# A doubling of lag factors on VectorE with the small power first, and its last step summed by transfers

## The chip, the cores and the metric

The kernel runs on one core of a Trainium2 chip. A core has TensorE (matrix products, with its weight loads shown apart as PEld), VectorE (DVE), ScalarE (ACT), GpSimd (POOL) and SyncE (SP, which issues most transfers). Each engine works through its own queue in order, and waits on semaphores for the others. The metric is the time of one execution on the device in microseconds (us); less is better.

## The reference, cut to what matters

Four layers follow one another on a sequence of 2048 rows of 512 channels: a long convolution, a gated feed-forward, and both once more. The convolution's filter is a sum over 128 states of powers of a complex number:

```
P = exp(logdA[:, :, None] * l)             # [512, 128, 2048], logdA = dt * A
K = einsum("dn,dnl,dn->dl", Cc, P, dB).real
y = irfft(rfft(u, 2L) * rfft(K, 2L))[:L] + u * Dskip
x = x + y
x = x + (silu(n @ w_gate) * (n @ w_up)) @ w_down     # n = layernorm(x)
```

The filter K depends on the weights alone. The kernel computes it once, for both convolutions.

## The kernel before, in words

**The chunk stage.** The filter is built for 8 chunks of 64 channels, with the 128 states on the partitions. A lag l is split as 32 a + s with a below 64 and s below 32. For each chunk the kernel makes two tables: `re` and `im` hold the complex powers in a (64 of them for each channel), `g` holds the 32 small powers in s, multiplied by the weight `w0` = C dt B. `lags` (L449) then multiplies them on TensorE, one small product per channel and part: 32 columns of `g` are the stationary operand, 64 columns of `re` or `im` the moving one, summed over the states. `spread_in`, `spread` and `spectra` (L460 to L518) turn the result into frequency weights: an eviction by ScalarE (L462), a rearranging product that also adds the row `dsk` of Dskip (L474), another eviction to `kt`, the spectral products (L493), their eviction (L502), sums on GpSimd (L504 to L514) and stores by SP (L516).

**The tables.** Sizes are exponentials on ScalarE (`gen_exp`, L384), among them five for the powers 1, 2, 4, 8, 16 of the small factor (`mz`, L389). Angles start on VectorE (`gen_turns`: L349 for 16 large multiples, L352 for the small powers), are rounded by ScalarE (`gen_reduce`: L360, L366), reduced on VectorE (L369, L372), and turned into sine and cosine on ScalarE (`gen_trig`: L379 to L381). `gen_e` (L401) puts `re` and `im` together on VectorE: L407 and L410 for one half, L413 and L416 for the other.

**The doubling.** `gen_g` (L419) multiplies the small factors `xr` and `xi` by their sizes (L424), makes the first factor (L427 to L431), and then doubles the table five times, for n = 1, 2, 4, 8, 16: entries n to 2n - 1 are entries 0 to n - 1 times the n-th power. Each doubling is a product with the real part (L437), one with the imaginary part into a scratch tile `tmp` (L441, at most 8 powers at a time, so twice for n = 16), a subtraction and an addition (L445, L446). `g` is laid out as [part, channel, power]: the 32 powers of a channel are neighbours.

**The order.** The order of the instructions on VectorE, ScalarE and TensorE is written out by hand for this stage: the steps are generators, and the text takes so many steps of each in turn (L850 on; the loop over chunks starts at `for i in range(NCH - 1)`). In turn i of the loop, VectorE makes `g` (`gg`) and the joined tables (`ge`) of chunk i + 1 and the angles (`tn`, `rd`) of chunk i + 2; ScalarE makes sines and exponentials of chunk i + 2 (`tr`, `ex`); TensorE makes the lag products and spectra of chunk i. It also forms norms of the feed-forward weights (`norm_units`, with the squares at L306 and the sums at L310) and the spectra of the second input block (`second`, L276, L279). In the last turn there is no chunk i + 2. The orders of SP's and GpSimd's queues, and of all engines behind this stage, come from a planner that simulates the kernel and issues an instruction when it thinks it is due.

**Buffers.** Tiles share memory by tag: a new tile of a tag waits for the readers of the old one. `bt` is the scratch of `tmp`, and later receives pieces of the feed-forward weights (L572); `t` holds `dsk` until the products of the convolution use it (L683). `W0` to `W3` hold `re` and `im` of even and odd chunks.

**Behind the stage.** The first block's convolution (`ssm`, L640, with `ei` products at L702), then for eight blocks the convolution of the next block on VectorE beside the feed-forward of this one on TensorE (L807 to L823).

Of the kernel before, what the change touches and what calls it, by code (L numbers as in the profile page):

```python
# [22 lines left out]
P = 128  # L23
# [13 lines left out]
NA = 21  # L37
# [7 lines left out]
def dft_constants():  # L45
# [17 lines left out]
    am[:, :5] = 2.0 ** np.arange(5)  # L63
    am[:, 5:] = 32.0 * np.arange(17, 33)
# [8 lines left out]
def kernel(ctx, tc, x, a_re, a_im, b_re, b_im, c_re, c_im, log_dt, d_skip,  # L73
# [25 lines left out]

    ldt = sb.tile([P, 4], F32, name="ldt")  # L100
# [65 lines left out]
    dt = tl([P, D], "dt", "bt")  # L166
# [3 lines left out]
    def gen_w():  # L170

        wt = tl([P, 2, D], "wt", "bt")
# [6 lines left out]
    dsk = tl([1, D], "dsk", "t")  # L179
# [154 lines left out]
    mz2 = tl([P, 2, 5, DC], "mz2", "y1")  # L334

    def gen_tiles(ch):
        re = tl([P, DC, 65], "re", f"W{2 * (ch % 2)}")
        im = tl([P, DC, 65], "im", f"W{2 * (ch % 2) + 1}")
        mu = tl([P, DC, 32], "mu", "n")
        xz = tl([P, 5, DC], "xr", "bb"), tl([P, 5, DC], "xi", "dd")  # L340
        mz = mz2[:, ch % 2]
        t16 = tl([P, DC, 16], "t16", "z")
        return re, im, mu, xz, mz, t16

    def gen_turns(ch, ts):
# [3 lines left out]
        V.tensor_tensor(t16, am[:, 5:].unsqueeze(1).to_broadcast([P, DC, 16]),  # L349
                        t_.unsqueeze(2).to_broadcast([P, DC, 16]), OP.mult)  # L350
        yield
        V.tensor_tensor(xz[1], am[:, :5].unsqueeze(2).to_broadcast([P, 5, DC]), t_.unsqueeze(1).to_broadcast([P, 5, DC]), OP.mult)  # L352
# [31 lines left out]
    def gen_exp(ch, ts):  # L384
# [3 lines left out]
        for lv in range(5):  # L388
            A.activation(mz[:, lv], r_, AF.Exp, scale=float(1 << lv))  # L389
# [29 lines left out]
    def gen_g(ch, ts, g):  # L419
# [6 lines left out]
        tmp = tl([P, 2, DC, 8], "tmp", "bt")  # L426
        V.tensor_tensor(g[:, :, :, 0], w_, re[:, :, 64].unsqueeze(1).to_broadcast([P, 2, DC]), OP.mult)  # L427
        V.tensor_tensor(tmp[:, :, :, 0], w_[:, ::-1], im[:, :, 64].unsqueeze(1).to_broadcast([P, 2, DC]), OP.mult)
        yield
        V.tensor_tensor(g[:, 0, :, 0], g[:, 0, :, 0], tmp[:, 0, :, 0], OP.subtract)  # L430
        V.tensor_tensor(g[:, 1, :, 0], g[:, 1, :, 0], tmp[:, 1, :, 0], OP.add)  # L431
        for n in (1, 2, 4, 8, 16):
            yield
            lv = n.bit_length() - 1
            zr, zi = (t[:, lv].unsqueeze(1).unsqueeze(3) for t in xz)
            new = g[:, :, :, n:2 * n]
            V.tensor_tensor(new, g[:, :, :, 0:n], zr.to_broadcast([P, 2, DC, n]), OP.mult)  # L437
            step = min(n, 8)
            for b0 in range(0, n, step):
                tmp = tl([P, 2, DC, 8], "tmp", "bt")[:, :, :, :step]  # L440
                V.tensor_tensor(tmp, g[:, ::-1, :, b0:b0 + step], zi.to_broadcast([P, 2, DC, step]), OP.mult)  # L441
                if b0 + step == n:
                    yield
                o = new[:, :, :, b0:b0 + step]
                V.tensor_tensor(o[:, 0], o[:, 0], tmp[:, 0], OP.subtract)  # L445
                V.tensor_tensor(o[:, 1], o[:, 1], tmp[:, 1], OP.add)  # L446
        yield

    def lags(ts, g):  # L449
        re, im = ts[:2]  # L450
        pk = pbig([P, 16, 64], "pk")
        for d in range(DC):
# [3 lines left out]
            PE.matmul(o, lhsT=g[:, 0, d], rhs=re[:, d, 0:64], start=True, stop=False, tile_position=(0, 32 * grp))  # L456
            PE.matmul(o, lhsT=g[:, 1, d], rhs=im[:, d, 0:64], start=False, stop=True, tile_position=(0, 32 * grp))
# [388 lines left out]
    with tc.manual_schedule(engines={mybir.EngineType.Activation, mybir.EngineType.DVE, mybir.EngineType.PE}):  # L846
# [18 lines left out]
        gs[0] = tl([P, 2, DC, 32], "g", "ga")  # L865
# [33 lines left out]
        for i in range(NCH - 1):  # L899
# [6 lines left out]
            gs[i + 1] = tl([P, 2, DC, 32], "g", ("gb", "ga")[i % 2])  # L906
# [6 lines left out]
            take(gg, 1)  # L913
            take(tn, 1)
            take(gg, 1)
            take(tn, 1)
# [3 lines left out]
            take(gg, 1)  # L920
            take(ge, 1)
            take(gg, 1)
            take(ge, 1)
            take(gg, 1)
            take(ge, 1)
            take(gg, 1)
            take(ge, 1)
            take(gg, 1)
# [167 lines left out]
```

## Time and profile before

| | before |
|---|---|
| median of 3 runs | 1214.09 us (1213.27 to 1214.4) |
| the profiled execution | span 1210.1 us, from first to last instruction; no other time is given for it |
| TensorE busy | 1104.0 us, 91% |
| VectorE busy | 1048.5 us, 87% |
| ScalarE busy | 646.3 us, 53% |
| GpSimd busy | 187.8 us, 16% |

The runs' time is that of the whole execution; what lies around the span (start and end) is in the first row and not in the second. Shares are averages over the whole span, and the stages have different limits. In rows of a profile, `L441` is a line of the kernel, `tmp<-g,xi` output and inputs, `128x1024` partitions and elements, `x6` a count; behind the first bar stand busy us and mean ns of one, behind the second the engine's idle time just before these instructions. In rows of a timeline, the first number is the start, the second the length in us, and a bracket at the end names an idle time and what ended it.

### The profile page before, as it was taken

Reading aid. Unit: us, or ns where it says so; the run is one execution under the profiler, and the core shown is the slowest. Engines: PE = TensorE matmul, PEld = TensorE weight load, DVE = VectorE, ACT = ScalarE, POOL = GpSimd, SP = SyncE. Lnnn points to the kernel's source line nnn. Section 1 sums busy time; section 2 is a strip of 40 time slices with the busy share of each in tenths; the row PEclk is TensorE's granted clock in tenths of the full one; section 3 lists DMA queues with packets and bytes.
Section 4 is the critical chain, followed back from the end, with each engine's and each line's share of the span. In section 5 each row is a group of like instructions: output and inputs, shape, how many; then the busy total and the mean of one; then the engine's idle time right before and its main releaser. Section 6 shows DMA issues by size and latency. Waiting matters only on the chain.

```text
span 1210.1 us, 25368 instructions
## 1 busy us (share of the span) xinstructions
PE 1104.0 (91%) x10220; PEld 858.5 (71%) x10220; DVE 1048.5 (87%) x1677; ACT 646.3 (53%) x1392; POOL 187.8 (16%) x209
## 2 busy tenths in 40 slices
PE   3877988888978998989999999999999999999998
PEld 2755766666976776868686777778686776867875
DVE  8999999999869999999998999999992799983221
ACT  7999999973265545526753524664431553324111
POOL 1116343453220010101100000121000010000000
PEclk9999998889999999999999999999999999999999
DMA  6223233236389427433245353424433144311000
GB/s 226 96 88 92 72 89 86 73 107 184 116 285 264 127 67 199 133 118 88 62 157 140 105 179 133 125 79 146 140 118 129 33 119 132 117 58 44 14 23 18
DMA packets 134857, 138.66 MB, mean 115 GB/s; under 512 B 75921, under 2 KB 85137, under 8 KB 134738
## 3 DMA queue, kind: packets, MB, share of 16 engines
q1 hardware_dynamic: 132178, 128.64, 35.4%
q0 software_dynamic: 2560, 8.39, 2.0%
q8 instruction: 80, 1.31, 0.5%
q14 instruction: 39, 0.32, 0.1%
HBM read 98.71 MB, written 28.31 MB: 105 GB/s over the span
## 4 chain that ended last, share of the span: by engine, by line
DVE 32%; PE 27%; issue 5%; DMA 4%; ACT 2%; POOL 2%; SPq 1%; DVEq 0%; ACTq 0%; POOLq 0%
DVE t L683 5%; PE pgu L807 5%; PE pgu L808 5%; PE pgu L809 5%; DVE yk L686 4%; DVE z L216 3%; DVE yk L683 3%; PE py L821 3%; PE py L822 3%; PE py L823 3%; PE pi L702 2%; DVE sg L813 2%; DVE hl L815 1%; DVE yl L216 1%; DVE bt L216 1%
## 5 line engine op out<-in xcount | busy, mean ns | idle before, releaser
L807 PE MATMUL pgu<-mix,wsl 128*128 128x256 f16 x1280 | 350.5, 274 | 7.9 <-DVE sg L813 4.4
L809 PE MATMUL pgu<-mix,wsl 128*128 128x256 f16 x1280 | 350.5, 274 | 1.2 <-DVE wsl L579 1.2
L808 PE MATMUL pgu<-mix,wsl 128*128 128x256 f16 x1280 | 350.4, 274 | 0.0
L808 PEld LDWEIGHTS <-wsl 128*128 128x128 f16 x1280 | 125.8, 98 | 24.6 <-issue 8.6
L821 PE MATMUL py<-wsl,hh 128*128 128x512 f16 (+1 forms) x352 | 134.6, 382 | 9.3 <-DVE xg L826 5.3
L809 PEld LDWEIGHTS <-wsl 128*128 128x128 f16 x1280 | 125.8, 98 | 16.5 <-DVE wsl L579 1.5
L807 PEld LDWEIGHTS <-wsl 128*128 128x128 f16 x1280 | 125.8, 98 | 15.8
L823 PE MATMUL py<-wsl,hl 128*128 128x512 f16 (+1 forms) x352 | 134.4, 382 | 2.4 <-DVE hl L815 2.4
L812 ACT ACTIVATE sg<-pgu,sc 128x512 f32<-128x512 f32 x80 | 54.5, 682 | 128.8 <-PE pgu L809 110.9
L822 PE MATMUL py<-wsl,hh 128*128 128x512 f16 x320 | 122.1, 382 | 0.0
L683 DVE TENSOR_TENSOR t<-uu,w 128x1024 f32<-128x1024 f32 x96 | 116.8, 1217 | 5.5 <-DMA uu<-udr 5.3
L686 DVE TENSOR_TENSOR yk<-yk,t 128x1024 f32<-128x1024 f32 x96 | 116.7, 1215 | 0.1
L493 PE MATMUL pw<-kt,ek 128*128 128x256 f32 (+2 forms) x420 | 105.4, 392 | 0.0
L813 DVE SCALAR_TENSOR_TENSOR sg<-pgu,sc,sg 128x512 f32<-128x512 f32 x80 | 59.6, 744 | 52.3 <-ACT sg L812 52.0
L702 PE MATMUL pi<-yl,mix 128*128 128x256 f16 x672 | 91.4, 273 | 5.5 <-ACT yl L691 3.5
L493 PEld LDWEIGHTS pw<-kt,ek 128*128 128x128 f32 x420 | 83.9, 208 | 11.9
L814 ACT ACTIVATE hh<-sg 128x512 f16<-128x512 f32 x80 | 50.0, 626 | 67.6 <-DVE sg L813 67.6
L211 POOL TENSOR_TENSOR rs<-mv,mhalf 128x2 f32<-128x2 f32 (+1 forms) x21 | 38.7, 1845 | 275.7 <-ACT mv L210 275.6
L260 PE MATMUL pf<-z,eh 128*128 128x256 f16 x576 | 74.4, 272 | 1.6 <-ACT z L250 1.6
L702 PEld LDWEIGHTS <-mix 128*128 128x128 f16 x672 | 65.3, 98 | 14.3 <-issue 3.9
L691 ACT ACTIVATE yl<-mix,sy 128x512 f16<-128x512 f32 x56 | 40.2, 717 | 61.4 <-DVE mix L688 61.2
L504 POOL COPY w0r<-s 128x128 f32<-128x128 f32 x29 | 48.1, 1659 | 141.7 <-ACT s L502 122.2
(221 smaller groups left out, 2292.0 us busy)
## 6 DMA issues: line engine op xcount, KB each, us to landing
w<-wdr SPq DMA_DIRECT2D x96, 256.0 KB, 2.8
uu<-udr SPq DMA_DIRECT2D x96, 256.0 KB, 3.0
udr<-u POOLq DMA_DIRECT2D x32, 256.0 KB, 2.8
wdr<-wo SPq DMA_DIRECT2D x96, 64.0 KB, 2.0
udr<-u SPq DMA_DIRECT2D x16, 256.0 KB, 2.5
n<-ndr SPq DMA_DIRECT2D x16, 256.0 KB, 3.0
n<-xdr SPq DMA_DIRECT2D x4, 1024.0 KB, 6.0
xg<-in_A_u_dram SPq DMA_DIRECT2D x3, 1024.0 KB, 7.4
```

The source lines that it names most:

```text
L260: PE.matmul(pf[:, o], lhsT=e, rhs=m, start=k == 0, stop=k == len(terms) - 1)
L493: PE.matmul(pw[:, i], lhsT=e, rhs=kt[:, :, c + 4 * k0:4 * k1:4, :].rearrange("p g k d -> p k g d"), start=c == 0, stop=c == 3)
L683: V.tensor_tensor(t, uu.unsqueeze(1).to_broadcast([P, 2, 2, HD]), w.unsqueeze(2).to_broadcast([P, 2, 2, HD]), OP.mult)
L686: V.tensor_tensor(yk, yk, t, OP.add)
L702: PE.matmul(pi[:, o], lhsT=e, rhs=m, start=k == 0, stop=k == len(terms) - 1)
L807: PE.matmul(o, lhsT=wgu(wi, k, 0)[:, fs], rhs=nh[:, k], start=k == 0, stop=False)
L808: PE.matmul(o, lhsT=wgu(wi, k, 0)[:, fs], rhs=nlo[:, k], start=False, stop=False)
L809: PE.matmul(o, lhsT=wgu(wi, k, 1)[:, fs], rhs=nh[:, k], start=False, stop=k == 3)
L813: V.scalar_tensor_tensor(sg, pgu[:, 1], sc6[:, 4:5], sg, OP.mult, OP.mult)
L821: PE.matmul(py[:, r], lhsT=hh[:n, f, rc], rhs=wd(f, 0)[:n], start=f == 0, stop=False)
L822: PE.matmul(py[:, r], lhsT=hh[:n, f, rc], rhs=wd(f, 1)[:n], start=False, stop=False)
L823: PE.matmul(py[:, r], lhsT=hl[:n, f, rc], rhs=wd(f, 0)[:n], start=False, stop=f == FT - 1)
```

## The change

- `g` is laid out as [part, power, channel]: the 64 channels of a power are neighbours. `lags` reads its 32 stationary columns with a step of 64 elements.
- The small factors are made for the powers 1, 2, 3, 4, 8, 16, six in place of five, so that entries 1 to 3 come from entry 0 in one step. The doublings for 4 and 8 are as before, each with one product into the scratch.
- In the last doubling VectorE makes the four products, one of them with the sign turned, two in `g` and two in scratch tiles; the additions are made by two accumulating transfers that GpSimd issues, 16 powers of 64 channels on 128 partitions each.
- The scratch is one tile `btl` for the whole stage, with `dsk` in a part of it that is free; a second scratch `th_` lies in the tag `t`; `dt` lies in `W3`.
- VectorE's order in the loop is changed: all but the last steps of `g` come early, mixed with the first four steps of `ge`; the last four steps of `ge` come at the end of each turn.

```diff
-NA = 21
+ZP = (1, 2, 3, 4, 8, 16)
+NZ = len(ZP)
+NA = NZ + 16
...
+    btl = tl([P, 7 * HD], "btl", "bt")
...
-    dt = tl([P, D], "dt", "bt")
+    dt = tl([P, D], "dt", "W3")
...
-    dsk = tl([1, D], "dsk", "t")
+    dsk = btl[0:1, 4 * HD:6 * HD]
...
+    tmp = btl[:, :4 * HD].rearrange("p (i s d) -> p i s d", i=2, s=8), tl([P, 16, DC], "tmp", "t")
...
-        for lv in range(5):
-            A.activation(mz[:, lv], r_, AF.Exp, scale=float(1 << lv))
+        for lv, m in enumerate(ZP):
+            A.activation(mz[:, lv], r_, AF.Exp, scale=float(m))
...
+        tm, th_ = tmp
...
+        zr, zi = (t[:, :3].unsqueeze(1).to_broadcast([P, 2, 3, DC]) for t in xz)
+        V.tensor_tensor(g[:, :, 1:4], g[:, :, 0:1].to_broadcast([P, 2, 3, DC]), zr, OP.mult)
+        V.tensor_tensor(tm[:, :, :3], g[:, ::-1, 0:1].to_broadcast([P, 2, 3, DC]), zi, OP.mult)
+        yield
+        V.tensor_tensor(g[:, 0, 1:4], g[:, 0, 1:4], tm[:, 0, :3], OP.subtract)
+        V.tensor_tensor(g[:, 1, 1:4], g[:, 1, 1:4], tm[:, 1, :3], OP.add)
+        for n in (4, 8):
+            yield
+            zr, zi = (t[:, ZP.index(n)].unsqueeze(1).unsqueeze(1).to_broadcast([P, 2, n, DC]) for t in xz)
+            V.tensor_tensor(g[:, :, n:2 * n], g[:, :, 0:n], zr, OP.mult)
+            V.tensor_tensor(tm[:, :, :n], g[:, ::-1, 0:n], zi, OP.mult)
+            yield
+            V.tensor_tensor(g[:, 0, n:2 * n], g[:, 0, n:2 * n], tm[:, 0, :n], OP.subtract)
+            V.tensor_tensor(g[:, 1, n:2 * n], g[:, 1, n:2 * n], tm[:, 1, :n], OP.add)
+        yield
+        zr, zi = (t[:, NZ - 1:].to_broadcast([P, 16, DC]) for t in xz)
+        V.tensor_tensor(g[:, 1, 16:], g[:, 1, :16], zr, OP.mult)
+        V.tensor_tensor(th_, g[:, 0, :16], zi, OP.mult)
+        G.dma_start(g[:, 1, 16:], th_, accum_op=OP.add)
+        yield
+        tl_ = tm.rearrange("p i s d -> p (i s) d")
+        V.tensor_tensor(g[:, 0, 16:], g[:, 0, :16], zr, OP.mult)
+        V.scalar_tensor_tensor(tl_, g[:, 1, :16], -1.0, zi, OP.mult, OP.mult)
+        G.dma_start(g[:, 0, 16:], tl_, accum_op=OP.add)
         yield
...
-            PE.matmul(o, lhsT=g[:, 0, d], rhs=re[:, d, 0:64], start=True, stop=False, tile_position=(0, 32 * grp))
-            PE.matmul(o, lhsT=g[:, 1, d], rhs=im[:, d, 0:64], start=False, stop=True, tile_position=(0, 32 * grp))
+            PE.matmul(o, lhsT=g[:, 0, :, d], rhs=re[:, d, 0:64], start=True, stop=False, tile_position=(0, 32 * grp))
+            PE.matmul(o, lhsT=g[:, 1, :, d], rhs=im[:, d, 0:64], start=False, stop=True, tile_position=(0, 32 * grp))
...
+            for g in (gg, gg, ge, gg, ge, gg, gg, rd, rd, ge, rd, rd, ge, rd, rd, rd, rd):
+                take(g, 1)
             while tops:
                 tops.pop(0)()
             take(sp, 1)
+            take(gg, 2)
             kp = spread(i, ks)
...
+            take(gg, 2)
...
-                take(ge, 2)
+                take(ge, 4)
                 take(gg, 1)
-                take(ge, 2)
```

71 lines of the change are left out of this document (17 added, 54 removed).

## The prediction

> **What bounds the kernel now.** I read the page's slices first, to find the stage that the change touches, then busy time by stage, then who waits for whom. The digits are tenths of 40 equal slices of about 30 us.
>
> ```profile
> DVE  8999999999869999999998999999992799983221
> ACT  7999999973265545526753524664431553324111
> ```
>
> VectorE and ScalarE are both full in the first eight or nine slices, which is the chunk stage, up to about 288 us. Behind it TensorE's feed-forward work fills the span, and the change doesn't touch that. So the stage is cut in three: two early chunks, five repeating ones, and the last one, which prepares no further chunk.
>
> ```profile
> core 0: us, PE busy (x) PEld busy (x) DVE busy (x) ACT busy (x) POOL busy (x), PEclk, DMA share, GB/s
> 24.45:88.16 63.71, 53.36 (x484) 43.39 (x484) 63.32 (x100) 63.40 (x168) 5.95 (x8) 0.95 0.26 88
> 88.16:259.02 170.86, 143.78 (x1915) 111.20 (x1914) 170.39 (x230) 158.22 (x410) 82.57 (x74) 0.91 0.30 81
> 259.02:288.17 29.15, 24.85 (x441) 19.51 (x443) 28.88 (x38) 13.13 (x39) 15.90 (x13) 1.00 0.44 127
> ```
>
> VectorE is never idle: 63.32 of 63.71, 170.39 of 170.86, 28.88 of 29.15 us. That is why work taken from it should shorten the stage. But ScalarE is as full in the first stretch (63.40), and has only 170.86 - 158.22 = 12.64 us free in the second. What it waits for there sets how much can be won:
>
> ```profile
> ACT ks L462 <- PE pk L457: 10.7, 3, 8.1
> ACT re L379 <- DVE im L372: 6.3, 4, 2.2
> ...
> ACT xr L379 <- DVE xi L369: 2.2, 3, 0.8
> ACT sq L306 <- DMA st<-in_B_w_down_dram: 1.8, 1, 1.8
> ```
>
> Columns: total us, times, longest. VectorE makes ScalarE wait 6.3 + 2.2 = 8.5 us. The 10.7 us for the lag products are mostly the last chunk's 8.1, behind this stretch. A faster VectorE can give back the 8.5 and no more: beyond that ScalarE is the bound.
>
> **VectorE's doublings.** Per chunk the doubling loop runs these, in an early chunk that GpSimd hardly disturbs:
>
> ```profile
> L441 DVE TENSOR_TENSOR tmp<-g,xi 128x1024 f32<-128x1024 f32 (+3 forms) x6 | 5.1, 849 | 0.0
> L437 DVE TENSOR_TENSOR g<-g,xr 128x128 f32<-128x128 f32 (+4 forms) x5 | 5.0, 993 | 0.0
> ...
> L446 DVE TENSOR_TENSOR g<-g,tmp 128x512 f32<-128x512 f32 (+3 forms) x6 | 3.0, 498 | 0.0
> L445 DVE TENSOR_TENSOR g<-g,tmp 128x512 f32<-128x512 f32 (+3 forms) x6 | 3.0, 498 | 0.0
> ```
>
> That is 6 x 0.849 + 5 x 0.993 + 12 x 0.498 = 16.0 us in 23 instructions. They overlap a little: one of 1.21 us is followed 1.13 us later, so each costs its duration less about 0.075.
>
> ```profile
> 71.93 1.21 DVE L437 TENSOR_TENSOR g<-g,xr 128x1024 f32<-128x1024 f32 x1
> 73.06 1.21 DVE L441 TENSOR_TENSOR tmp<-g,xi 128x1024 f32<-128x1024 f32 x1
> ```
>
> So 16.0 - 23 x 0.075 = 14.3 us. The new prices by size:
>
> ```profile
> L445 DVE TENSOR_TENSOR g<-g,tmp 128x512 f32<-128x512 f32 x3 | 2.0, 682 | 0.0
> ...
> L445 DVE TENSOR_TENSOR g<-g,tmp 128x256 f32<-128x256 f32 x1 | 0.4, 406 | 0.0
> ...
> L445 DVE TENSOR_TENSOR g<-g,tmp 128x128 f32<-128x128 f32 x1 | 0.3, 276 | 0.0
> ...
> L445 DVE TENSOR_TENSOR g<-g,tmp 128x64 f32<-128x64 f32 x1 | 0.3, 260 | 0.0
> ```
>
> Between 512 and 1024 elements an element costs (1210 - 682) / 512 = 1.03 ns, so 384 take about 0.55 us, and 192 lie between 0.276 and 0.406, at 0.34. First three powers in one step: 2 x 0.55 + 2 x 0.34 = 1.78. Power 4: 2 x 0.68 + 2 x 0.41 = 2.18. Power 8: 2 x 1.21 + 2 x 0.68 = 3.78. Power 16: four products of 1024, 4.84, its four adds being left to transfers (I price the product that also negates like the others; its form at that size isn't in these rows). Sum 12.58, less 16 x 0.075, is 11.4. The sixth power adds 64 elements to four instructions (both products with the sizes, the turns at L352, the reduction at L369): 4 x 64 x 1.03 ns = 0.26. Saved: 14.3 - 11.4 - 0.26 = 2.6 us a chunk, 13 us over the five repeating chunks. The two multiplications and two adds of the first factor stay; their g is now contiguous, a gain of at most 0.1 us that I leave out.
>
> **ScalarE's share.** One more exponential per chunk, and 64 elements more in four instructions (L360, L379, L380, L381).
>
> ```profile
> L366 ACT ACTIVATE re<-t 128x1024 int32<-128x1024 f32 x1 | 1.1, 1085 | 0.0
> L389 ACT ACTIVATE mz<-rho 128x64 f32<-128x64 f32 x5 | 0.8, 242 | 0.0
> ```
>
> The five together are busy 0.8 us, overlapping, and one alone takes 0.24, so another adds (0.8 - 0.24) / 4, about 0.15; 64 elements are at most 1085 / 1024 x 64 = 0.07 us. Together 0.15 + 4 x 0.07 = 0.4 a chunk, 3.2 for eight, all of it on a full engine. ScalarE thus reaches the last chunk 8.5 - 3.2 = 5.3 us earlier. VectorE alone would be 13 us earlier there; it will wait for ScalarE instead, and the new order lets it: the reductions that ScalarE's sines need come before the step of power 8, so neither of the two waits above should be left.
>
> **The last chunk** sets what follows, because all of the tail starts with its lag products.
>
> ```profile
> 281.63 2.22 DVE L413 SCALAR_TENSOR_TENSOR im<-im,mu 128x1984 f32<-128x1984 f32 x1
> ...
> 285.48 2.77 DVE L416 TENSOR_TENSOR re<-re,mu 128x992 f32<-128x992 f32 x2
> ```
>
> ```profile
> 284.65 1.24 PE L493 MATMUL pw<-kt,ek 128*128 128x256 f32 x5
> ```
>
> ```profile
> 287.19 0.33 PE L456 MATMUL pk<-re,g 128*32 128x64 f32 x7 [1.30 <-DVE re L416]
> ```
>
> TensorE is through with its earlier work at 285.9 and waits 1.3 us for VectorE. Both ends move: TensorE's by the 5.3 us of ScalarE that feeds it, to 280.6; VectorE's by 5.3 and its own 2.6, from 288.2 to 280.3. So the first product could start at 280.6, 6.6 us earlier.
>
> **The transfers.** Two of 512 KB per chunk, issued by GpSimd, 4 KB per partition, within the chip's memory, adding as they write. The trace has none that adds; the rows nearest in size and issuer:
>
> ```profile
> udr<-u POOLq DMA_DIRECT2D x32, 256.0 KB, 2.8
> ...
> x<-in_A_u_dram SPq DMA_DIRECT2D x1, 1024.0 KB, 9.5
> ...
> st<-in_B_w_down_dram SPq DMA_DIRECT2D x1, 512.0 KB, 6.7
> ```
>
> ```profile
> L637 POOL DMA_DIRECT2D udr<-u x32: 539/540/810, 430.9 to 890.5; - x32
> ```
>
> Issue costs GpSimd 0.54 us, of which it has plenty (82.57 busy of 170.86); queued behind the waiting issue are memsets and copies of the next spectra, which ScalarE feeds later anyway. Landing: below 2.8 us nothing, 9.5 if reading the destination counts like twice the bytes, more if the second queues behind the first. I take 6.7, the same size. After the second issue VectorE still has 2.22 + 2.77 = 5.0 us of L413 and L416, so in the last chunk it lands at 280.3 - 5.0 + 6.7 = 282.0: 1.4 us later than TensorE could start. Start 282.0 against 287.2: 5.2 us won. In the repeating chunks VectorE, being ahead, has more room, and I cost the landing at nothing there. If it is late in one, the lag products, ScalarE's L462 behind them and everything queued on it wait. VectorE gets a wait too: the next chunk's second step writes the scratch that the second transfer still reads, some 5.0 + 2 us behind its issue; were it late, the next turns (L352) and ScalarE's rounding of them stand behind it. A landing of 6.7 us fits.
>
> The page "DMA: Bandwidth & Descriptors" of the Trainium skill (Anatomy of one DMA, SWDGE path) fits a GpSimd-issued transfer by 2.0 us plus bytes over 436 GB/s; for 512 KB that is an estimate of 3.2 us, by which the last start would be the 280.6 and the gain 6.6. No run here shows it for an adding transfer.
>
> **Weight loads of the lag products.** g now lies with the power outside and the channel inside, so each load of 32 columns reads with a step of 64 elements instead of 32 neighbours. Nothing like it runs on TensorE now.
>
> ```profile
> L457 PEld LDWEIGHTS pk<-im,g x128: 107/109/110, 192.0 to 197.1; 128*32 128x32 f32 x128
> L457 PE MATMUL pk<-im,g x128: 217/218/221, 192.1 to 197.2; 128*32 128x64 f32 x128
> ```
>
> ```profile
> L493 PEld LDWEIGHTS pw<-kt,ek 128*128 128x128 f32 x420 | 83.9, 208 | 11.9
> ```
>
> ```profile
> 197.59 1.02 ACT L462 ACTIVATE ks<-pk 128x1024 f32<-128x1024 f32 x1
> ```
>
> A load costs (208 - 109) / 96 = 1.03 ns a column, 33 ns for 32. The chunk has 256 loads (L456 and L457) in four column groups in about 5.4 us, 84 ns for each of a group's 64. 256 x 33 ns would be 8.4 us, so they already run beside each other. On VectorE the step shows: 64 single elements take 260 ns, 128 in pairs 276, double per element. If TensorE's loads double too, the added 33 ns is hidden in the 84 (0 us), or exposed within each group (64 x 33 ns = 2.1 us a chunk), or, with no overlap at all, 8.4 us. I take 0, since the loads overlap now; a gain has no reason. The room is small: the products end at 197.4, and ScalarE takes them at 197.6.
>
> The page "SBUF — State Buffer" of the Trainium skill (Door 1) says that each access to a new 16-byte line pays, unless a line is hit at least twice. The two VectorE rows agree. Applied to the weight loads it is the third rival.
>
> **At nothing.** dt in the buffer of an early imaginary part: its readers come before the first write in VectorE's order. The skip row now shares the scratch buffer that the first weight piece is loaded into, so that load waits for the last chunk's spread:
>
> ```profile
> 287.96 0.56 SPq L572 DMA_DIRECT2D st<-in_B_w_gate_dram  x1
> ```
>
> ```profile
> 317.30 2.76 ACT L573 ACTIVATE wsl<-st,sc 128x1376 f16<-128x1376 f32 x2
> ```
>
> It is issued at 288.0 and used at 317.3. Some 10 us later there is still room; beyond that, every load queued on SP behind it is late.
>
> **The sum.** Span 1210.1 - 5.2 = 1204.9. The profile gives no time of its own for that execution beside the span; the median of the runs, 1214.09, is 4.0 above it, and I keep that: 1208.9 us. A change under 0.2%, 2.4 us, can't be told from none.
>
> **Rivals.**
>
> First, more is won: ScalarE's other waits go too (1.8 for the load, and some 1.5 for TensorE). For it speaks the clock: after a pause of 4.13 us six of the next products take 2.77 us, after one of 1.08 us they take 1.46, and with ScalarE's lost waits that pause gets shorter.
>
> ```profile
> 219.11 1.21 PE L310 MATMUL nrm<-sq,onesb 128*128 128x344 bf16 x3 [4.13 <-ACT sq L306]
> ...
> 220.96 2.77 PE L493 MATMUL pw<-kt,ek 128*128 128x256 f32 x6
> ```
>
> ```profile
> 151.10 1.07 PE L310 MATMUL nrm<-sq,onesb 128*128 128x344 bf16 x3 [1.08 <-ACT sq L306]
> ...
> 152.44 1.46 PE L493 MATMUL pw<-kt,ek 128*128 128x256 f32 x6
> ```
>
> Then 5.3 + 3.3, and the last landing hidden as well (1.3 us of TensorE's wait): 9.9, and 1204.2.
>
> Second, transfers land late. In the last chunk the start is 275.3 plus the landing; at 11.9 us it is the old 287.2 and nothing is won: 1214. That needs two adding transfers to run one behind the other at about twice the plain price. Between 9.5 and 14.3 us the result is within 2.4 us.
>
> Third, slower: the strided loads are exposed, 2.1 us a chunk. The five repeating chunks each lose 2.1 - 0.2 on ScalarE's full queue, the last 2.1: 11.6 against 5.2 won, +6.4, 1220.5. It decides from the x with 6x - 1.0 = 5.2, about 1.0 us a chunk; at the full 8.4 us it would be far slower, which I give no weight, since the loads overlap now. Against it: the overlap, and the shorter pause of the first rival, which gives the products room.
>
> **How the numbers follow.** Forecast 0.50, first rival 0.14, second 0.14, third 0.22. Faster is the first two, 0.64; same the second rival, 0.14; slower the third, 0.22. The forecast alone spans 1207.5 to 1212: TensorE's 280.6 with no landing in the way, or a landing of 9.5 us. The range takes in the three other cases, 1202.5 to 1219.5, and leaves out the third's outer half.
>
> **What would show it.** Right: VectorE with idle time in the chunks and waits on ScalarE; ScalarE without waits for L369 and L372's counterparts; four 1024-element products at the last doubling; landings near 6.7 us. Wrong: lag products above 6 us, or ScalarE waiting for them in each chunk (third rival); TensorE or ScalarE waiting for the transfers (second); VectorE still never idle (then its new order costs more than counted).

## The result and the profile after

The kernel after takes 1199.8 us (median of 4 runs, 1195.8 to 1203.8) where the kernel before takes 1214.2 (median of 4, 1213.3 to 1217.0): a ratio of 0.987, 95% interval 0.985 to 0.990. Repeated among the last runs of the study, it is 0.990, interval 0.986 to 0.993. One execution of the study, the second of g1, took 4603 us and is left out of every figure below. The direction was forecast; the size, 1208.9 with a range down to 1202.5, was not.

The slices of the page of the kernel after:

```profile
DVE  7988999996979998999999999999993899983211
ACT  6999999982256544636654533745432552224111
```

VectorE is no longer full in every slice of the chunk stage; ScalarE still is. Line numbers behind the edits have moved: the copy of the lag products into ks, L462 before, is L476 now, the lag products are L470 and L471, and the two transfers are L455 and L460. I use the copy of the lag products as the milestone of each chunk, because ScalarE, the full engine, makes it once a chunk. Its starts, first in the kernel before, then after, first, second, seventh and eighth chunk:

```profile
65.83 1.00 ACT L462 ACTIVATE ks<-pk 128x1024 f32<-128x1024 f32 x1
97.04 1.00 ACT L462 ACTIVATE ks<-pk 128x1024 f32<-128x1024 f32 x1
...
266.21 1.02 ACT L462 ACTIVATE ks<-pk 128x1024 f32<-128x1024 f32 x1 [1.06 <-PE pk L457]
294.70 1.02 ACT L462 ACTIVATE ks<-pk 128x1024 f32<-128x1024 f32 x1 [8.11 <-PE pk L457]
```

```profile
68.68 1.00 ACT L476 ACTIVATE ks<-pk 128x1024 f32<-128x1024 f32 x1
101.25 1.00 ACT L476 ACTIVATE ks<-pk 128x1024 f32<-128x1024 f32 x1
...
260.22 1.02 ACT L476 ACTIVATE ks<-pk 128x1024 f32<-128x1024 f32 x1 [0.30 <-PE pk L471]
288.93 1.02 ACT L476 ACTIVATE ks<-pk 128x1024 f32<-128x1024 f32 x1 [5.79 <-PE pk L471]
```

In this profile the first chunk is 2.85 us later than before, the second has lost another 1.36, then the five repeating chunks win 10.2, and the last wins nothing. Net, the stage ends 5.8 us earlier. Busy time in the five repeating chunks, in the last chunk and behind the last copy, before and after (columns as in the prediction):

```profile
97.04:266.21 169.17, 141.79 (x1907) 109.47 (x1906) 168.66 (x229) 155.51 (x406) 80.38 (x71) 0.91 0.31 84
266.21:294.70 28.49, 22.78 (x368) 17.79 (x369) 27.90 (x34) 6.99 (x13) 17.36 (x15) 1.00 0.50 138
294.70:1210.10 915.40, 874.85 (x7185) 678.29 (x7185) 761.00 (x1258) 396.11 (x746) 74.37 (x91) 0.99 0.39 118
```

```profile
101.25:260.22 158.97, 139.51 (x1900) 108.09 (x1899) 153.94 (x194) 157.50 (x411) 70.74 (x80) 0.94 0.51 121
260.22:288.93 28.71, 23.02 (x368) 18.28 (x369) 25.35 (x34) 7.01 (x12) 14.39 (x16) 1.00 0.76 201
288.93:1199.10 910.17, 872.20 (x7185) 676.72 (x7185) 755.32 (x1246) 396.68 (x746) 70.85 (x91) 0.99 0.39 118
```

ScalarE (the fourth figure) is idle for 169.17 - 155.51 = 13.66 us of the five chunks before and for 1.47 after. It has 1.99 us more to do, just the forecast 0.4 a chunk. So 12.2 us of idle time came back, less 2.0 of work: the 10.2. VectorE, never idle before, now has 158.97 - 153.94 = 5.03 us to spare. The waits from 20 to 300 us (total, times, longest) say the same from both sides:

```profile
ACT sq L309 <- DMA st<-in_B_w_up_dram: 7.6, 1, 7.6
...
DVE xi L373 <- ACT xr L364: 6.3, 3, 2.6
...
DVE im L376 <- ACT re L370: 1.7, 4, 0.4
```

VectorE waits for ScalarE's roundings, and ScalarE's longest wait is one for a weight load, in the last chunk. Behind the stage this execution shows another 5.2 us (915.40 to 910.17), which I had not forecast at all. Most of the experiments went into that.

The two doubtful parts: the transfers in the page's list of DMA issues (KB, median us to landing), the second one by its line (ns to issue: least, median, most; then who waited for it), and the weight loads by their tile.

```profile
g<-tmp POOLq DMA_DIRECT2D x8, 512.0 KB, 4.6
g<-btl POOLq DMA_DIRECT2D x8, 512.0 KB, 5.9
```

```profile
L460 POOL DMA_DIRECT2D g<-btl x8: 851/860/872, 50.9 to 271.4; - x8
...
PE pk L470: 2.7, 1
```

```profile
L471 PEld LDWEIGHTS pk<-im,g x1024: 131/143/155, 56.6 to 288.6; 128*32 128x32 f32 x171
```

The adding transfers land after 4.6 and 5.9 us (medians; at most 8.5 and 8.9) and are waited for once, 2.7 us, by the first chunk's lag products. A strided weight load takes 143 ns instead of 109.

### The profile page after: what moved, and what is told of

It reads as the page before. It is cut to its first block, busy times and chain, and to the rows that moved or that the text cites. A ratio compares the mean times of both kernels' runs of the same rounds, so it can differ in the third digit from the quotient of the medians.

```text
span 1199.1 us, 25374 instructions
## 1 busy us (share of the span) xinstructions
PE 1102.7 (92%) x10220; PEld 857.4 (72%) x10220; DVE 1022.5 (85%) x1621; ACT 650.4 (54%) x1400; POOL 176.4 (15%) x225
## 4 chain that ended last, share of the span: by engine, by line
PE 46%; DVE 17%; issue 4%; DMA 3%; ACT 2%; POOL 1%; SPq 1%; DVEq 0%; ACTq 0%; POOLq 0%
PE pgu L821 8%; PE pgu L822 8%; PE pgu L823 8%; PE py L835 5%; PE py L837 5%; PE py L836 5%; PE pi L716 4%; PE pf L263 4%; DVE t L697 2%; DVE yk L700 2%; DVE yk L697 2%; DVE z L219 2%; DMA mix<-nn 1%; DVE sg L827 1%; DVE bt L219 1%
## 5 line engine op out<-in xcount | busy, mean ns | idle before, releaser
L507 PE MATMUL pw<-kt,ek 128*128 128x256 f32 (+2 forms) x420 | 102.0, 382 | 0.0
L507 PEld LDWEIGHTS pw<-kt,ek 128*128 128x128 f32 x420 | 81.5, 202 | 10.9
L214 POOL TENSOR_TENSOR rs<-mv,mhalf 128x2 f32<-128x2 f32 (+1 forms) x21 | 35.2, 1675 | 246.7 <-ACT mv L213 246.7
L836 PEld LDWEIGHTS <-hh 128*128 128x128 f16 (+1 forms) x352 | 34.7, 99 | 48.4 <-issue 13.5
```

Source lines behind the costliest of these rows:

```text
L507: PE.matmul(pw[:, i], lhsT=e, rhs=kt[:, :, c + 4 * k0:4 * k1:4, :].rearrange("p g k d -> p k g d"), start=c == 0, stop=c == 3)
L836: PE.matmul(py[:, r], lhsT=hh[:n, f, rc], rhs=wd(f, 1)[:n], start=False, stop=False)
```

## The experiments

**Does the order behind the stage make the other half?** The stage's order on VectorE, ScalarE and TensorE is written out in the program; behind it the planner lays out all engines from its own estimate of when the stage ends. Comparing the instructions of the two built programs shows that it came to different orders, on ScalarE and VectorE among others. My theory was that the second half of the gain was this order. The rival was that all of it comes with the stage. A few useless instructions at the end of the stage shift the planner's estimate, and with the right number of them either kernel gets, instruction for instruction on all five engines, the order of the other. First filler, on ScalarE (the number differs):

```
         i = NCH - 1
+        for _ in range(50):
+            A.activation(dmy, dmy, AF.Copy)
         pk = lags(ts[i], gs[i])
```

> The kernel before, with 50 small copies (32 elements each, of a scratch tile, useless) queued on ScalarE ahead of its copy of the last chunk's lag products. Their one purpose is that the planner, which sees the chunk stage end later, lays out what lies behind the stage in exactly the order that it has in the kernel after, on all five engines; in the stage itself nothing else is changed. On the chip a small activation in a row takes about 0.156 us (19 of 64 elements in 2.96 us), so 50 take 7.8 us, inside the 8.1 us that ScalarE waits there. Theory (the planner's other order of the feed-forward part gave the second half of the gain): the copy of the last lag products stays at 294.7 us, and from there to the end of the span it takes about 910 us as in the kernel after, not 915: span about 1205, time about 1207. Rival (the second half comes with the changed stage itself, its buffers and transfers): 915 us behind the copy, span 1210, time about 1212 to 1214.

> The kernel after with the same 50 useless copies on ScalarE; the planner's order behind the stage stays that of the kernel after. ScalarE waits only 5.8 us there, so up to 2 us of the 7.8 shows. Theory and rival alike: copy of the last lag products at 289 to 291 us, 910 us behind it, span 1199 to 1201, time about 1201 to 1203. Against the run of the kernel before with the same copies and the same order, it shows the stage's own gain alone: by the theory 3.5 to 6 us, by the rival about 11.

> The kernel after with 35 such copies, 5.5 us on ScalarE inside its wait of 5.8 us. With this number the planner lays out everything behind the stage in exactly the order of the kernel before. Theory: copy of the last lag products at 289 us, then about 915 us as in the kernel before: span about 1204, time about 1206. Rival: 910 us behind the copy, span 1199, time about 1200.

> The kernel before with 25 such copies, 3.9 us inside ScalarE's wait of 8.1 us; the order behind the stage stays that of the kernel before. It tells what the useless copies themselves do. Theory and rival alike: copy of the last lag products at 294.7 us, 915 us behind it, time 1212 to 1216, as the kernel before. If it moves by several us, the copies are no neutral filler and the other three runs have to be read by their traces alone.

Measured, against the kernel before: 1.002 (0.999 to 1.005), 0.994 (0.992 to 0.996), 0.991 (0.988 to 0.994) and 0.998 (0.995 to 1.000). The theory's first forecast failed: with the order of the kernel after, the kernel before takes 1216.2 us. Its forecast for e3 came true: 1206.2 us, for 1206. But the filler was not neutral, so these four decide nothing. One copy, in place on the same tile, costs 0.26 us, not 0.156; in e1 and e2 the copy of the last lag products stood behind it. ScalarE's timeline in e1:

```profile
291.29 13.02 ACT L1000 ACTIVATE dmy<-dmy 128x32 f32<-128x32 f32 x50
304.22 1.01 ACT L464 ACTIVATE ks<-pk 128x1024 f32<-128x1024 f32 x1
```

So the filler went to VectorE, behind its last work for the lag products, where it later waits for TensorE anyway:

```
         i = NCH - 1
+        for _ in range(23):
+            V.memset(dmy, 0.0)
         pk = lags(ts[i], gs[i])
```

> The kernel before with 23 useless fills of 32 elements queued on VectorE behind its last work for the last chunk's lag products, so that they hold up neither these products nor ScalarE; the planner then lays out what lies behind the stage in exactly the order of the kernel after. The earlier filler on ScalarE cost 0.26 us a copy and pushed the stage's end itself; this one should leave the copy of the last lag products at 294 to 295 us. Theory (the order is worth some us of the part behind the stage): at equal mean granted clock 3 to 5 us below the kernel before, part behind the copy 911 to 912 us at a clock of 0.98. Rival (the order is worth nothing): as the kernel before within 1.5 us, 915 us behind the copy.

> The kernel after with the same 23 fills on VectorE, order behind the stage as in the kernel after. Copy of the last lag products at 288 to 289 us, about 911 us behind it, time as the kernel after. Against the kernel before with the same fills and order it gives the stage's own part of the gain, by the theory 5 to 7 us at equal clock; by the rival (all of the gain comes with the stage) 10 to 12.

> The kernel after with 35 such fills on VectorE, with which the planner lays out what lies behind the stage in exactly the order of the kernel before. Copy of the last lag products at 288 to 289 us. Theory: 3 to 5 us above the kernel after with its own order at equal clock, 914 to 916 us behind the copy. Rival: no different from it within 1.5 us.

f1 took 1214.8 us, 0.9995 of the kernel before (0.997 to 1.002): the order of the kernel after gives the old stage nothing. f2 took 1199.3 (0.987, 0.983 to 0.992) and f3 1203.2 (0.989, 0.985 to 0.992): their intervals overlap, and four runs each could not tell 4 us from none. So the question was asked again with more runs on one chip, beside the kernel after itself, and with a third order, which 29 fills bring about:

> The kernel after as it is, on the chip and among the runs of the other three, so that they are compared with it directly: 1198 to 1204 us by either theory, 10 to 16 below the kernel before.

> The kernel after with 35 useless fills on VectorE behind its last work for the lag products, which give it the order of the kernel before behind the stage, now in five rounds beside the kernel after. Theory (the planner's order is a part of the gain, given the new stage): 2 to 5 us above the kernel after, 914 to 917 us behind the last copy of the lag products. Rival (what lies behind the stage only scatters from run to run): within 1.5 us of it.

> The kernel after with 29 such fills, with which the planner comes to a third order behind the stage, different from both kernels'. It shows how much such an order is worth by itself. Theory (the order decides some us): a time that differs from the kernel after by 2 us or more, in either direction, with an equal stage. Rival: within 1.5 us of it.

The kernel after took 1200.1 us (0.990, 0.986 to 0.993), the same with the order of the kernel before 1200.0 (0.990, 0.987 to 0.992). My theory has fallen: these two orders are worth the same. The third took 1195.0 (0.985, 0.982 to 0.989). Where that came from, the order or a stage that happened to end earlier, the last pair was to show; its second kernel also moves squares, as told below:

> The kernel before with 26 useless fills on VectorE behind its last work for the lag products, which give it, behind the stage, the third order that was 5 us faster with the new stage. If the order itself is worth that, it comes here too: about 5 us below the kernel before, 910 to 912 us behind the last copy of the lag products. If it is not, and the 5 us were the stage's shorter end (283.1 us against 286.3) and scatter: within 2 us of the kernel before.

> The kernel after with the four squares of the last chunk moved and 30 fills that give the third order behind the stage: both edits that came out fastest. If each has its own effect, 3 us from the first and 5 from the second: 1191 to 1194 us. If both only took the same wait of ScalarE in the last chunk away (in the run with the third order that wait for the load did not occur): 1195 to 1197.

h1 took 1206.0 us, 0.993 of the kernel before (0.990 to 0.995), with its stage unchanged: the third order is itself worth 9.4 us to the old stage by the medians, and 5 us by the stretch behind the last copy in the two profiles (910.4 against 915.4). h2 took 1196.3 (0.985, 0.982 to 0.989), so the two edits don't add up. An order behind the stage can thus decide more than the whole edit was forecast to bring, but the two that this change swapped are equal.

With orders matched, the change is worth 1214.8 - 1199.3 = 15.5 us in the order of the kernel after (f1, f2, one chip). In the order of the kernel before it is worth 11.7 and 12.7 (f3 and g3, each against the kernel before itself on the same chip). In the third order it is 1206.0 - 1195.0 = 11.0 (h1 and g4), or 8.3 with the 2.7 us by which the kernel before differs between their chips. For that pair the stretches from the eighth copy to the end, h1 first:

```profile
265.69:295.24 29.55, 22.77 (x368) 17.79 (x369) 27.26 (x55) 7.00 (x13) 15.48 (x15) 1.00 0.58 161
295.24:1205.60 910.36, 872.85 (x7185) 678.33 (x7185) 761.51 (x1264) 396.53 (x746) 73.19 (x91) 0.99 0.39 117
```

```profile
257.69:283.11 25.42, 22.75 (x368) 18.01 (x368) 23.05 (x50) 6.98 (x14) 12.82 (x16) 1.00 0.76 211
283.11:1193.20 910.09, 873.36 (x7185) 678.13 (x7185) 760.44 (x1261) 396.38 (x746) 70.49 (x91) 0.99 0.40 118
```

The stage ends 12.1 us earlier, and what lies behind takes the same 910 us. And a second profile of the very kernel after, g2, puts its gain elsewhere than the first did (last chunk, then what lies behind):

```profile
258.26:286.25 27.99, 23.32 (x368) 18.38 (x368) 26.14 (x35) 7.01 (x13) 12.99 (x16) 0.99 0.76 202
286.25:1201.90 915.65, 876.21 (x7185) 679.31 (x7185) 755.45 (x1246) 396.89 (x746) 70.87 (x91) 0.99 0.39 117
```

8.5 us in the stage, and behind it 915.65, nothing less than before. The 5.2 us behind the stage in the first profile are not steady. A part of such differences goes with TensorE's clock, which the traces have granted either in full or by half: behind the eighth copy it is half for 19.1 us in the kernel before, for 14.2 in the first profile of the kernel after, 24.8 in g2 and 34.5 in f1. Over the 20 profiles of the study, 10 us more at half go with 4.4 us more behind the stage (correlation 0.72).

**Which engine is the bound now?** Two kernels make one instruction of each chunk twice, to the same result: ScalarE's rounding of 128x1024, and VectorE's crosswise product of power 8. Both, like the two after them, carry fills that keep the order behind the stage.

```
             A.activation(k, src, AF.Copy, scale=1.0 / st)
+            if st == 1:
+                A.activation(k, src, AF.Copy, scale=1.0 / st)
```

> The kernel after with ScalarE's largest rounding of a chunk's turns (128x1024, 1.09 us) made twice, to the same result, in every chunk; 34 useless fills on VectorE behind its last work for the lag products keep the order behind the stage that of the kernel after. From the second chunk's copy of the lag products to the seventh's (five chunks) the kernel after takes 158.97 us, with ScalarE idle for 1.47 of them and VectorE for 5.03. Theory (ScalarE is now the bound): five times 1.09, so 164 to 165 us for the five, and 6 to 8 us more in time than the kernel after. Rival (VectorE still sets the pace): below 161 us, time within 2 us of the kernel after.

```
             V.tensor_tensor(tm[:, :, :n], g[:, ::-1, 0:n], zi, OP.mult)
+            if n == 8:
+                V.tensor_tensor(tm[:, :, :n], g[:, ::-1, 0:n], zi, OP.mult)
```

> The kernel after with the crosswise product of power 8 (128x1024, 1.21 us) made twice on VectorE, to the same result, in every chunk, and the same 34 fills behind the last chunk. Theory (ScalarE is the bound, VectorE has 1.0 us a chunk to spare): 159 to 161 us for the five chunks, time 0 to 3 us above the kernel after. Rival (VectorE still sets the pace): five times 1.21, 165 us, and 6 to 8 us more in time.

The five repeating chunks of p1, then of p2:

```profile
101.57:265.93 164.36, 138.86 (x1898) 107.44 (x1897) 153.82 (x193) 162.79 (x416) 66.45 (x80) 0.95 0.49 116
```

```profile
101.54:272.36 170.82, 138.90 (x1900) 109.32 (x1899) 159.39 (x197) 157.23 (x412) 67.87 (x82) 0.94 0.48 117
```

p1 does as ScalarE's theory says: 158.97 + 5 x 1.09 = 164.4, and 164.36 measured; 1208.8 us in time (0.994, 0.991 to 0.997). p2 went past both forecasts: 170.8, with VectorE idle for 11.4 us. What it waits for is a transfer. The timeline of p2's fourth chunk:

```profile
151.07 1.22 DVE L463 SCALAR_TENSOR_TENSOR btl<-g,xi 128x1024 f32<-128x1024 f32 x1
...
154.81 0.86 POOL L522 COPY w0r<-s 128x128 f32<-128x128 f32 x1 [3.63 <-ACT s L520]
155.64 2.42 POOL L528 TENSOR_TENSOR wo<-s 128x192 f32<-128x192 f32 x2
...
158.00 0.86 POOL L464 DMA_DIRECT2D g<-btl  x1
...
162.95 0.40 DVE L434 TENSOR_TENSOR btl<-w,im 128x128 f32<-128x128 f32 x1 [2.95 <-DMA g<-btl]
162.96 0.19 PEld L474 LDWEIGHTS pk<-re,g 128*32 128x32 f32 x2 [5.88 <-issue]
162.99 0.48 PE L474 MATMUL pk<-re,g 128*32 128x64 f32 x5 [5.51 <-DMA g<-btl]
```

The second scratch is ready at 152.3, but its transfer is issued at 158.0: GpSimd's queue is not part of the order written out, and the planner, seeing VectorE 1.2 us later, put a copy and one or two combinations of a spectrum between the two transfers, in three of the chunks. In the two repeating chunks where it did not, the kernel takes 32.76 and 31.57 us, against 32.35 and 31.34 in f2 (32.67 and 31.45 in the kernel after). So VectorE's 1.2 us nearly vanish there, as the theory says, but the run as a whole is no test of it, since it moved a second thing. Time 1213.9 us (0.998, 0.996 to 1.000).

**What do the transfers and the new order bring?**

```
-        G.dma_start(g[:, 1, 16:], th_, accum_op=OP.add)
+        V.tensor_tensor(g[:, 1, 16:], g[:, 1, 16:], th_, OP.add)
...
-        G.dma_start(g[:, 0, 16:], tl_, accum_op=OP.add)
+        V.tensor_tensor(g[:, 0, 16:], g[:, 0, 16:], tl_, OP.add)
```

> The kernel after with the last doubling's two sums made by VectorE instead of the accumulating transfers: two additions of 128x1024 a chunk, some 1.2 us each by the products of that size; 20 fills behind the last chunk keep the order behind the stage that of the kernel after. Theory (VectorE has 1.0 us a chunk to spare): of the 2.4 us a chunk some 1.4 show, 164 to 167 us for the five chunks; the first chunk's lag products no longer wait 2.7 us for a transfer. Time 4 to 8 us above the kernel after. Rival (the transfers are worth nothing, since what they save waits for ScalarE or for their landing): below 161 us for the five, time within 2 us.

For the other kernel the steps of the repeating and last chunks are taken in the old order:

```
-            for g in (gg, gg, ge, gg, ge, gg, gg, rd, rd, ge, rd, rd, ge, rd, rd, rd, rd):
-                take(g, 1)
+            take(gg, 1)
+            take(ge, 1)
...
+            take(gg, 1)
+            take(rd, 1)
...
-            take(gg, 2)
+            take(gg, 1)
+            take(rd, 1)
+            take(gg, 1)
+            take(rd, 3)
...
-                take(ge, 4)
+                take(ge, 2)
                 take(gg, 1)
+                take(ge, 2)
```

> The kernel after with the order in which VectorE's steps are taken in the repeating and last chunks put back to that of the kernel before, everything else of the change kept; 48 fills behind the last chunk keep the order behind the stage that of the kernel after. Theory (the new order is needed for ScalarE to be kept busy): the reductions come behind the step of power 8 again, ScalarE waits for them 1 to 2 us a chunk as before, 163 to 167 us for the five chunks, time 4 to 8 us above the kernel after. Rival (the shorter doublings alone do it): below 161 us, ScalarE's waits for VectorE below 2 us in all.

The five repeating chunks of p3, and waits in those of p4:

```profile
102.20:270.14 167.94, 139.72 (x1907) 108.58 (x1906) 166.87 (x203) 158.02 (x411) 69.47 (x70) 0.95 0.31 83
```

```profile
ACT re L385 <- DVE im L378: 19.6, 5, 4.3
...
DVE im L413 <- ACT re L403: 9.2, 4, 2.8
...
DVE re L416 <- ACT mu L403: 6.6, 5, 1.7
```

With VectorE adding, it is full again (166.87 of 167.94) and the time is the old one: 1216.9 us, 1.000 (0.998 to 1.003). The transfers carry 9 us of the five chunks, more than the theory's 5 to 8, and by the time practically the whole gain: 13 to 16 us of it (1.000 against 0.987 and 0.990), where the theory had 4 to 8. The first chunk's copy does not come earlier without them: it stands at 70.4 us, not 68.7. With the old order the transfers, layout and three-power step make the kernel slower than before: 1221.0 us, 1.005 (1.003 to 1.006), five chunks in 178.7 us, ScalarE waiting 19.6 for the reductions, and VectorE in turn 9.2 and 6.6 for ScalarE's squarings: the two wait for each other, by more than forecast.

**What sets the last chunk's end?** In the kernel after, ScalarE waits 7.6 us at the fourth square of a weight piece, and the evictions that TensorE needs stand behind it. The timeline of that kernel:

```profile
273.20 2.28 DVE L420 TENSOR_TENSOR re<-re,mu 128x992 f32<-128x992 f32 x2
...
278.14 0.49 ACT L309 ACTIVATE sq<-st 128x344 bf16<-128x344 f32 x1 [7.63 <-DMA st<-in_B_w_up_dram]
278.53 1.07 ACT L516 ACTIVATE s<-pw 128x512 f32<-128x512 f32 x2
...
282.37 0.37 PE L470 MATMUL pk<-re,g 128*32 128x64 f32 x8
```

VectorE is through with the stage at 275.5; the first lag product starts at 282.4.

n1 takes one square a step earlier; g1, shown here, also takes the other three behind the evictions:

```
+            if not more:
+                norm_units(1, 9)
             kt = kt2[:, i % 2]
...
-        norm_units(4, 9)
-        take(sp, 2)
         norm_units(0, 0)
-        take(sp, 3)
+        take(sp, 5)
+        norm_units(3, 9)
...
         pk = lags(ts[i], gs[i])
+        norm_units(0, 0)
```

> The kernel after with one of the last four squares of the weight sizes moved a step ahead on ScalarE, in front of its copy of the chunk's spread products, where it waits 2.7 us anyway; the order behind the stage stays that of the kernel after, without any filler. In the kernel after ScalarE waits 7.6 us for that square's load, behind which its evictions of the spectra, TensorE's further products and with them the last lag products stand. Theory: that wait sets the start of the last lag products, so they start 3 to 5 us earlier, the copy at 284 to 286 us, time 3 to 5 us below the kernel after. Rival: the last accumulating transfer is then what ends last (issued at 271.5 us, landing up to 8.9 us): start at 280.4 us at the earliest, a gain of at most 2 us, with TensorE waiting for the transfer.

> The kernel after with the last chunk's four squares of the weight sizes taken off the way: one a step earlier in front of a copy for which ScalarE waits anyway, three behind its evictions of the spectra, and TensorE's products of them behind the last lag products instead of ahead of them. The order behind the stage is that of the kernel after. Theory (in the last chunk ScalarE's wait of 5 to 8 us at the fourth square sets the start of the last lag products): from the seventh copy of the lag products to the eighth it takes 24 to 26 us, not 28.7; time 2 to 4 us below the kernel after in the same call. Rival (the last accumulating transfer ends at the same time): 27 us or more, with TensorE waiting for the transfer, and no gain in time.

n1 takes 25.7 us for the last chunk, 3 less than the first profile of the kernel after, but its last copy comes at 286.9, not at 284 to 286; g1 takes 27.3, not the 24 to 26 of its theory. In n1 ScalarE still waits 5.5 us, for TensorE's product of an earlier square. n1 takes 1199.1 us (0.986, 0.983 to 0.989), where f2, the kernel after with fills, has 1199.3 on the same chip. g1 takes 1196.8 (0.987, 0.983 to 0.990), where the kernel after has 1200.1 (0.990, 0.986 to 0.993) on its chip. That is within the intervals, so a gain isn't shown. The wait is also not steady: it was 5.2 to 8.5 us for the load in five profiles of this stage with the four squares in place, and in f2, g3 and g4 it was 5.1 for TensorE's product. With the load waited for, the last chunk takes 28.0 to 30.4 us (the first profile, f3, g2; no filler on ScalarE); without, 25.1 to 27.3 (f2, g3, g4, n1, g1, h2). So the load costs about 3 us there when it comes late. The lowest median of the study is g4's, not clear of h2's and g1's.

## Why the prediction was wrong

**The step that failed** is "A faster VectorE can give back the 8.5 and no more: beyond that ScalarE is the bound." ScalarE is the bound, as p1 shows, but its waits came to more than the two lines that I added up. In the five repeating chunks alone it was idle for 13.66 us, of which 12.2 came back: besides the 8.5 for VectorE the 1.8 for a load and 1.1 of the lag products, and the rest in pieces too small for the list of waits. I had the figure in front of me, 170.86 - 158.22 = 12.64, and put only the named waits into the sum. The first rival, that ScalarE's other waits go too, happened; I gave it 0.14.

**The first two chunks** were costed at ScalarE's new work alone, 0.8 us for two, and lost 2.85 + 1.36 = 4.2. TensorE's wait of 2.7 us for a transfer in the first is not the reason: its products still start earlier than before, at 56.5 us for 57.1, and the copy of them, at 68.7, waits for nothing. ScalarE itself is late. From the timelines of the first chunk, before and after:

```profile
45.79 0.76 DVE L372 SCALAR_TENSOR_TENSOR im<-t,re 128x128 f32<-128x128 f32 x3
46.46 2.29 DVE L437 TENSOR_TENSOR g<-g,xr 128x2048 f32<-128x2048 f32 x1
...
57.05 0.33 PE L456 MATMUL pk<-re,g 128*32 128x64 f32 x7 [4.08 <-DVE re L416]
```

```profile
49.37 1.22 DVE L459 SCALAR_TENSOR_TENSOR btl<-g,xi 128x1024 f32<-128x1024 f32 x1
...
50.50 0.75 DVE L376 SCALAR_TENSOR_TENSOR im<-t,re 128x128 f32<-128x128 f32 x3
...
51.28 1.12 ACT L383 ACTIVATE re<-im 128x1024 f32<-128x1024 f32 x1 [1.05 <-DVE im L376]
...
56.47 0.40 PE L470 MATMUL pk<-re,g 128*32 128x64 f32 x3 [2.68 <-DMA g<-btl]
```

The order of steps ahead of the loop was not changed, but `g` has fewer steps now, so the last reductions of the second chunk's angles come behind the products of power 16 and no longer ahead of them. ScalarE waits 1.3 us for reductions there (3.8 in p3, where VectorE also adds). Up to the second copy it is idle for 2.7 us more than before: these 1.3, 0.7 for a product of TensorE, and 0.7 at the start that g2 and g4 don't show. It also has 1.5 us more to do; it makes the tables of three chunks by then, not of two.

**The last chunk.** In that profile neither VectorE (through at 275.5, not 280.3) nor a transfer, but the weight load decided. The lag products started at 282.4, where I had 282.0, by another road: +10.2 and -4.2 for my 5.3, and a last chunk of the same length. The stage's end in that profile, 5.8 us earlier for the forecast 5.2, is thus right by cancellation. Over six profiles with the new stage (with no filler on ScalarE) the last copy stands at 283.1 to 288.9 us, 285.9 on average; over four with the old one at 294.7 to 295.3. On average the five chunks win 10.3 us, the first two lose 2.9 and the last wins 1.8: the stage's gain is 9 us, not 5.

**Behind the stage** I took nothing to change, and with matched orders nothing was shown to: 910.4 and 910.1 us in the third order; in the order of the kernel before 915.4 and 915.7 with the old stage, 914.8 and 912.5 with the new (f3, g3). Only in the order of the kernel after does the one undisturbed profile of the old stage stand apart: 919.5 (f1) against 910.2, 915.7 and 913.8, and in f1 the clock was at half for 34.5 us there, against 14.2, 24.8 and 21.1. What I left out is that the order there hangs on the stage's end through the planner. It did change, and happened to be worth nothing.

**The 4.0 us around the span** were not around it: the time is 1.8 us above the span in every run of the study. The rest was that the profiled execution before, 1210.1 + 1.8 = 1211.9, lies low among the executions of its kernel: 98 runs of it on four chips have a median of 1215.7, from 1207.6 to 1223.5. To keep the 4.0 did no harm to the difference, which is what a forecast should be made of: 5.2 us forecast, 14 measured.

What the runs don't settle is the rest between the 9 us of the stage and the 12 to 16 of the time in the two orders of these kernels (in the third, 8 to 11, there is none). The first profile of the kernel before was 3.8 us below the median of its runs, which is a part of it; those of e4, f1 and h1 were within 2 us of theirs. The mean granted clock is another candidate: 0.974 on average in the runs of the kernel before, 0.980 in those of the kernel after. But the clock inside the stage rose as well (0.91 to 0.94 in the five chunks), where TensorE isn't the bound, and that alone moves the mean by 159 x 0.03 / 1200 = 0.004.

**What was right:** VectorE's saving (168.66 - 153.94 = 14.7 us in five chunks for the forecast 13) and its new idle time, ScalarE's added 2.0 us in five chunks, the reductions' new place taking ScalarE's waits for them away (p4), and the transfers landing beneath VectorE's other work. The weight loads doubled their cost per column as taken, 109 to 143 ns, and the lag products of a chunk took 5.3 to 5.9 us in seven chunks and 6.5 in the last, where before they took 5.2 to 6.2 and 7.5: as forecast, nothing of it shows. Where the page "SBUF — State Buffer" of the Trainium skill (Door 1) says that every new 16-byte line pays, the load's row agrees; the third rival, that it would show in the time, did not come. The landing was 4.6 and 5.9 us where I took 6.7, and an issue 0.86 where I took 0.54. The estimate of 3.2 us by the Trainium skill's page "DMA: Bandwidth & Descriptors" (Anatomy of one DMA, SWDGE path) is below the median of both transfers; the measurement decides.

## What to carry to other kernels

What an engine can win back is its whole idle time in the repeating part, window less busy time, less its new work, and not the sum of its named waits; the first and the last turn of a loop are then costed by themselves, each with what ends last there. Moving work from a full engine paid here only together with the order that let the next full engine use it: the shorter doubling is a gain in the new order and a loss in the old. A step list that is left as it was changes its meaning when one of its generators gets fewer steps, and a queue that is left to the planner can put other work ahead of a transfer. Where a planner lays out what follows, compare at a matched order before the remainder of a difference is given a cause, and take more than one profile.

## What was unexpected of the hardware

One execution is a loose measure of this kernel. On one core, with the same program, 98 runs spread over 16 us, and they go with the mean clock granted to TensorE, 0.969 to 0.980: over all 240 runs of the study, kernel by kernel, 0.01 less clock goes with 8.0 us more span (95% interval 6.9 to 9.2). TensorE is busy for some 875 of the 915 us behind the stage, and 0.01 of that, as an estimate, would be 8.75. Why the clock differs from run to run these traces don't show.

A copy of 128x32 in place on ScalarE takes 0.26 us in a row of such copies (13.02 for 50), where 19 exponentials of 128x64 to different places took 0.156 each. In the first row each copy needs the one before; that this makes the difference is not shown, since the two rows differ in the function too. A filler is priced by a row of its own kind.
